# Four attention layers on one core: first heads scored from 16 rows of Q, and one layer's gate moved into the output weights

## Chip, cores and metric

The kernel runs on one core of a Trainium2 chip. A core has TensorE (PE in the tables, with PEld for its weight loads), VectorE (DVE), ScalarE (ACT), GpSimd (POOL) and SyncE (SP, which issues the DMAs), and each runs its own list of instructions. The metric is the time of one execution in microseconds of device time; lower is better.

## The reference

Input x is 2048 tokens by 512 features, one batch. Four layers follow each other, A, B, A, B, each as x = x + layer(layernorm(x)). Both kinds have 32 heads of 16 features.

- Layer B is plain attention over all 2048 tokens: softmax(q k^T / 4) v, then a product with the output weights.
- Layer A works in 4 segments of 512 tokens. Inside a segment it is causal attention. Beside it, a memory M (16 x 16 per head) and a vector z are summed over the earlier segments, and a gate g per head, the sigmoid of beta, mixes the two:

```python
logits = jnp.einsum('bhqd,bhkd->bhqk', qs, ks) * scale + mask
p = _softmax(logits, axis=-1)
a_dot = jnp.einsum('bhqk,bhkd->bhqd', p, vs)
pq = phi(qs)
num = jnp.einsum('bhld,bhde->bhle', pq, M)
den = jnp.einsum('bhld,bhd->bhl', pq, z)[..., None] + 1e-06
a_mem = num / den
o = g * a_mem + (1.0 - g) * a_dot
outs.append(o)
pk = phi(ks)
M = M + jnp.einsum('bhld,bhle->bhde', pk, vs)
z = z + jnp.einsum('bhld->bhd', pk)
```

## The kernel before

The program is a builder: Python code that writes out every engine's instruction list in advance, in an order chosen by a planner with its own costs (`Sched`). Layers are numbered 0 to 3; layers 0 and 2 are A, layers 1 and 3 are B.

**Scores and exponentials.** Heads are handled in groups. Q and K lie in SBUF with features on the partitions, 128 partitions (8 heads) to a channel block c, in QA and KA for A layers and QB and KB for B layers. The array of TensorE is used in four tiles of 32 rows; a tile r holds two heads of 16 features. A group is one segment of queries, one block c and e = 0 or 1, the first or the second head of every tile. To score one head from 32 rows, `select` makes a masked copy `qm` of the Q block, in which the rows of the other head are zero (line 1533); it runs on DVE for A groups and mostly on POOL for B groups. There are 6 such buffers (`NQM`), so three pairs. `unit` then writes two or three score tiles of 128 keys by 512 queries into PSUM banks and lets ACT take their exponential in one instruction of 1024 or 1536 columns into `pT` (line 1643). On the causal diagonal of A groups a mask is added by TensorE (tri, ident) or applied afterwards by POOL (line 1657).

**DVE takes a part of the exponentials.** For chosen score tiles, `dx_first` (line 1165) turns a tile of PSUM into a 16-bit integer that, read as bf16, is a rough power of two; two further passes (lines 1219 and 1236) make two shifted copies, and TensorE adds three products with V in place of one. The buffers for it are `dxt` and parts of KA, QA, VA, wA and wB that are not in use.

**Values.** `pv` multiplies the exponentials with V into one accumulator bank. For B groups the result is 17 rows per head (the 17th is the softmax's sum) in four column tiles of 32; DVE copies it (`ub`), a DMA transposes it (`tb`), and POOL divides it into `ob` (line 1788). For A groups DVE divides (line 1738). A DMA transposes `ob` into `oT`.

**Memory of A layers.** `task_mem` sums phi(K) V into M, then writes masked bf16 copies `Mn` and `Mz`, one instruction each for every block c (lines 884 and 886). For segments 1 to 3 it multiplies them with `phq`, the phi of Q, scales the result by g over the denominator (`amem`), and a DMA transposes it back into `phq`.

**Output of A layers.** `task_out` first gates: for every block c, DVE writes oT = oT * (1 - g) + phq in place (line 994; in segment 0, without memory, oT = oT * (1 - g), line 990). Then, for each of 4 row tiles, `mm_wide` multiplies the 4 blocks with the output weights `woA`, as 4 matmuls of 32 columns of the array each, and DVE adds the result to x (line 1009).

**Background work.** Projections, layer norms (`normalize`, line 695), memory, outputs and DVE's exponentials are tasks that the planner puts between the units of scores. Its limits come from the table `PLAN`, with one row for each stretch of 40 units. `evac` copies projections out of PSUM on DVE, or on ACT where DVE is planned to be late (lines 559 and 561). `keep_busy` and `fill_gaps` put products of a tile of zeros with woB into gaps of TensorE, so that its clock stays up; how much a running product counts for that is set by constants such as `ROW_TILE` and `ROW_FILL`.

Of the kernel before, what the change touches and what calls it, by code (L numbers as in the profile page):

```python
# [7 lines left out]
ALU = mybir.AluOpType  # L8

P = 128  # L10
S_TOK = 2048
D = 512
H = 32
NT = 16
NCH = 4
# [13 lines left out]
ROW_FILL, COL_FILL, COL_ANY, CLOCK = 0.33, 0.15, 0.71, 341  # L29

# [276 lines left out]
class Builder:  # L307
    STRETCH = 40
    PLAN = {
        0: dict(TAKEN_A=1, MASK_PE=800, PE_LOW=7, GAP=3, BG_BANK=400),  # L310
        1: dict(R_LATE=1200, BUSY_ROOM=300, CARRY_W=0, NEARW=40, PAIRS=999, LEVEL=3, TAKEN=0.5, DVE_LATE=1700, BUSY_BACK=800),
        2: dict(MARGIN=500, DX_BANK=900, NEAR=8, EARLY=300, FILL=0.42, CR_B=1200, PART=3, NEARW=20, PAIRS=60, DX_FIN=3000),
        3: dict(NEAR=8, TAKEN_A=1, PV_SKIP=900, BACK=8, CR_W=1900, NEARW=20, TAKEN=0.4, LOW=14, HOLD_AT=40, PHI_LATE=0),
        4: dict(R_LATE=1200, NEARW=40, PAIRS=24, LEVEL=3, TAKEN=0.5),
        5: dict(DX_LATE=700, SLACK=350, BACK=4, LEVEL=3, BUSY_WAIT=0, PE_LOW=7, DVE_LATE=1700),
        6: dict(NEAR=10, PV_SKIP=200, BACK=3, DX_LAG=3, MASK_PE=800, DIV_LATE=2500, BG_BANK=100, QUAD=0),
        7: dict(REST=10, SLACK=350, R_NEAR=10, EARLY=0, FILL_DVE=200, BUSY_ROOM=300, R_PAIRS=2, PAIRS=999, TAKEN=0.3, QWAIT=8, QMIN=4),
        8: dict(R_LATE=1200, BACK=2, CR_W=1300, NEARW=20, BUSY_WAIT=0, TAKEN=0.3, DVE_LATE=800, QWAIT=3, QMIN=4, HOLD_MAX=0, PHI_LATE=300),
        9: dict(ACT1=400, R_LATE=1200, DX_BANK=700, NEAR=18, CR_W=1900, CR_B=1800, R_PAIRS=2, PAIRS=24, DIV_LATE=800, DVE_LATE=800),
        10: dict(DX_LATE=500, NEAR=5, TAKEN_A=1, SLACK=250, CARRY_W=0, R_PAIRS=2, PAIRS=999, DIV_LATE=800, BUSY_WAIT=0, PE_LOW=4, DVE_LATE=800, BG_BANK=100, QUAD=0, HOLD_MAX=0, PHI_LATE=300),  # L320
        11: dict(DX_LATE=900, R_NEAR=10, BUSY_ROOM=900, FILL=0.42, OPART=4, MASK_PE=800, DIV_LATE=2500, DVE_LATE=800, QWAIT=3, QMIN=4, HOLD_SEGS=2, PHI_LATE=0, POOL_QM=1),
# [32 lines left out]
    PHI_LATE = 100  # L354
    LAG_M = 2
    LOOK, PV_TAKEN = 1, 1
    NQM = 6
    NEARW = 60
    WARM, WARM2 = 84, 20
    LAG_A = 2  # L360
# [1736 lines left out]
```

## Time and profile before

| | |
|---|---|
| median of 3 runs | 1741.07 us (1740.86 to 1743.66) |
| the profiled execution | 1743.75 us |
| its span, first to last instruction | 1742.0 us |
| mean granted TensorE clock in it | 0.998 |
| DVE, idle in the span | 12% |
| POOL, busy in the span | 10% |

The profile is of one execution. Busy time counts every moment in which an engine has at least one instruction running, so it can be less than the count times the mean length of one. The rows of the table by stage give, for each engine, busy us and the number of instructions, then the granted clock, the busy share of the DMA engines and GB/s. A row of the view of waits gives who waited, for whom, us in total, how often, and the longest. A row of the groups gives the line, the engine, the operation, what is written from what, the shapes, the count, then busy us, mean ns of one, and the idle time of the engine just before, with what ended it. A row of the timeline has the start and the length in us, and in brackets the idle time before it and its cause.

### The profile page before, as it was taken

To read this page: it belongs to the slowest core of one execution; us is meant where nothing else is said; L and a number is where in the kernel's file an instruction comes from. 1 tells how busy PE (TensorE), PEld (TensorE's weight loads), DVE (VectorE), ACT (ScalarE), POOL (GpSimd) and SP (SyncE) were. 2 spreads that over 40 slices of the span, in tenths; PEclk is the share of its full clock that TensorE was granted. 3 is DMA by queue.
4 is the path that set the end of the run, shared out by engine and by line. 5 is a ranking of instruction groups with operands and counts; after the bars stand their busy time and mean duration, and the time that the engine had idled before them with its cause. 6 is when DMAs were issued, how large, how long until landed. Compare 5 with 4: busy or idle time off the path is not lost.

```text
span 1742.0 us, 47805 instructions
## 1 busy us (share of the span) xinstructions
PE 1652.7 (95%) x19946; PEld 604.6 (35%) x19946; DVE 1527.2 (88%) x2977; ACT 1703.7 (98%) x1608; POOL 182.8 (10%) x292
## 2 busy tenths in 40 slices
PE   8999899999999899999999999999999999999999
PEld 5553335332222523522235222532222222222236
DVE  6758665999999688799998999889999999999996
ACT  7899999999999999999999999999999999999998
POOL 2310100111100300100002100110010100000000
PEclk9999999999999999999999999999999999999999
DMA  6110211001221221102202111010011001000010
GB/s 176 37 22 20 44 14 29 17 8 22 41 47 23 56 56 32 33 8 59 59 14 38 46 32 41 19 46 14 10 23 26 22 13 23 10 10 11 8 29 18
DMA packets 148440, 54.60 MB, mean 31 GB/s; under 512 B 128768, under 2 KB 147712, under 8 KB 148224
## 3 DMA queue, kind: packets, MB, share of 16 engines
q1 hardware_dynamic: 148224, 51.56, 13.9%
q8 instruction: 156, 2.56, 0.6%
q14 instruction: 60, 0.49, 0.1%
HBM read 18.88 MB, written 2.10 MB: 12 GB/s over the span
## 4 chain that ended last, share of the span: by engine, by line
ACT 43%; PE 36%; issue 11%; DVE 6%; DMA 2%; SPq 1%; POOL 1%; ACTq 0%; DVEq 0%; POOLq 0%
ACT pT L1643 42%; PE ps L522 35%; PE ps L2032 1%; SPq L568 1%; DVE KA L1165 1%; DMA tb<-ub 1%; DMA xT<-xn 1%; POOL pT L1657 1%; DVE dxt L1165 1%; ACT amem L762 0%; DVE wA L1165 0%; DVE lnst L667 0%; POOL qm L1533 0%; DMA phq<-amem 0%; DVE VB L561 0%
## 5 line engine op out<-in xcount | busy, mean ns | idle before, releaser
L1643 ACT ACTIVATE pT<-ps 128x1024 bf16<-128x1024 f32 (+1 forms) x1561 | 1670.8, 1239 | 25.3 <-PE ps L522 19.4
L522 PE MATMUL ps<-qm,KB 32*128 32x512 bf16 x4096 | 571.0, 384 | 56.2 <-ACT pT L1643 43.7
L522 PE MATMUL ps<-pT,VB 128*17 128x512 bf16 x2907 | 497.4, 384 | 1.5 <-DVE QB L561 0.3
L522 PEld LDWEIGHTS ps<-qm,KB 32*128 32x128 bf16 x4096 | 148.4, 91 | 561.0 <-ACT pT L1643 462.0
L1165 DVE TENSOR_SCALAR KA<-ps 128x512 uint16<-128x512 f32 (+1 forms) x453 | 315.3, 704 | 11.4 <-PE ps L522 7.6
L1165 DVE TENSOR_SCALAR dxt<-ps 128x512 uint16<-128x512 f32 (+1 forms) x315 | 220.7, 704 | 12.5 <-PE ps L522 9.7
L522 PEld LDWEIGHTS ps<-pT,VB 128*17 128x17 bf16 x2907 | 116.6, 87 | 287.5 <-issue 274.3
L522 PE MATMUL ps<-dxt,VB 128*17 128x512 bf16 x939 | 197.5, 381 | 0.0
L2032 PE MATMUL ps<-woB,zero 128*32 128x512 bf16 (+7 forms) x655 | 166.9, 295 | 0.0
L522 PE MATMUL ps<-QA,VB 128*17 128x512 bf16 x445 | 129.5, 382 | 0.0
L1165 DVE TENSOR_SCALAR wA<-ps 128x512 uint16<-128x512 f32 (+1 forms) x174 | 123.2, 718 | 3.6 <-PE ps L522 1.1
L1788 POOL TENSOR_TENSOR ob<-tb,rd 128x512 bf16<-128x512 bf16 x31 | 35.7, 1152 | 817.9 <-DVE rd L1784 762.4
L522 PE MATMUL ps<-VA,VB 128*17 128x512 bf16 x445 | 120.3, 381 | 0.0
L1657 POOL TENSOR_SCALAR_AFFINE_SELECT pT<-pT 128x256 bf16<-128x256 bf16 (+4 forms) x113 | 61.7, 561 | 480.8 <-ACT pT L1643 480.8
L522 PE MATMUL ps<-KA,VB 128*17 128x512 bf16 x445 | 109.7, 381 | 0.0
L522 PE MATMUL ps<-wA,VB 128*17 128x512 bf16 x555 | 109.0, 381 | 0.0
L522 PE MATMUL ps<-VA,pT 128*128 128x51 bf16 (+1 forms) x2540 | 104.2, 187 | 4.7 <-POOL pT L1657 2.3
L522 PE MATMUL ps<-qm,KA 32*128 32x128 bf16 (+2 forms) x1536 | 93.1, 255 | 12.8 <-ACT pT L1643 9.4
L522 PEld LDWEIGHTS ps<-VA,pT 128*128 128x128 bf16 x2540 | 89.6, 96 | 23.2 <-issue 7.6
L1533 POOL TENSOR_SCALAR qm<-QB,par 128x512 bf16<-128x512 bf16 x96 | 74.0, 780 | 217.6 <-PE ps L522 197.7
L522 PE MATMUL ps<-woB,zero 128*32 128x512 bf16 (+1 forms) x282 | 92.7, 381 | 0.0
L1165 DVE TENSOR_SCALAR wB<-ps 128x512 uint16<-128x512 f32 (+1 forms) x109 | 81.2, 749 | 3.3 <-PE ps L522 2.4
(165 smaller groups left out, 1979.7 us busy)
## 6 DMA issues: line engine op xcount, KB each, us to landing
wB<-in_B_wqkv_dram SPq DMA_DIRECT2D x48, 128.0 KB, 2.3
wA<-in_A_wk_dram SPq DMA_DIRECT2D x16, 128.0 KB, 2.2
wA<-in_A_wq_dram SPq DMA_DIRECT2D x16, 128.0 KB, 2.4
wA<-in_A_wv_dram SPq DMA_DIRECT2D x16, 128.0 KB, 2.5
out_dram<-x SPq DMA_DIRECT2D x8, 256.0 KB, 2.2
x<-in_A_x_dram SPq DMA_DIRECT2D x3, 512.0 KB, 9.8
wB<-in_B_wqkv_dram SPq DMA_DIRECT2D x1, 1536.0 KB, 12.5
oT<-ob SPq DMA_TRANSPOSE x63, 2.4
```

Source lines behind the costliest of these rows:

```text
L522: self.sc.add("pe", lambda e: e.matmul(out, lhsT, rhs, start=start, stop=stop, skip_group_check=True), reads=reads, banks=[(bank, "w", all ...
L568: t[2] = self.sc.add_dma("sp", lambda e: e.dma_start_transpose(out, in_), b, reads=reads, writes=writes, deps=list(deps) + ([t[2]] if t[2] ...
L1165: self.op("dve", lambda e: e.tensor_scalar(d, o, SCALE * LOG2E * 128, 127.0 * 128 + EXP_BIAS, op0=ALU.mult, op1=ALU.add), writes=[self.b_d ...
L1533: self.op(eng, (lambda m, q, col: lambda e: e.tensor_scalar(m, q, col, 0.0, op0=ALU.mult, op1=ALU.add))(m, q, col), reads=[bq, self.b_par] ...
L1643: self.sc.add("act", (lambda dst, src: lambda e: e.activation(dst, src, ACT.Exp, scale=SCALE))(dst, src), writes=self.b_pT[slot * 3 + i:sl ...
L1657: self.op("pool", (lambda blk, pat: lambda e: e.affine_select(blk, blk, pattern=pat, compare_op=ALU.is_ge, fill=0.0, base=0, channel_multi ...
L1788: self.op(eng, lambda e: e.tensor_tensor(ob, t[:, :, :, 0:16], rb, ALU.mult), reads=[br] + self.b_tb, writes=self.b_ob[oi], **(dict(ns=125 ...
L2032: new = Op("pe", 0, (lambda o, z, w: lambda e: e.matmul(o, z, w, start=False, stop=False, skip_group_check=True))(o, z, w), f"fill {cols} ...
```

## The change

1. The first head of each tile (e = 0) gets no masked copy: `scores` and `query` take its 16 rows of Q and of K directly. The second head still uses a copy and 32 rows. `NQM` goes from 6 to 3, and `select` from needing two free copies to needing one. Line numbers move by a few.
2. In layer 2, for blocks 0 to 2 (`NG`), the gate is folded into a scaled copy `woG` of the output weights, made once by DVE. The memory part `phq` of these blocks is no longer added by DVE, but multiplied with `woA` by TensorE into the same accumulation: 7 products per row tile in place of 4 in segments 1 to 3. Block 3 of layer 2 and all of layer 0 stay as they were.
3. `Mn` and `Mz` are written for two blocks c per instruction.
4. 39 of the 40 rows of `PLAN` are replaced, some with settings that no row had before, such as `POOL_XN` (normalization on POOL) in six of them. Only the first row is shown.

```diff
+GATED, NG = 2, 3
...
-        0: dict(TAKEN_A=1, MASK_PE=800, PE_LOW=7, GAP=3, BG_BANK=400),
...
+        0: dict(R_LATE=2200, DX_LATE=500, DX_BANK=900, REST=16, NEAR=18, R_NEAR=50, PV_SKIP=200, CR_W=1900, CR_B=1800, RGAP=2, R_PAIRS=2, PAIRS=24, MASK_PE=800, DIV_LATE=800, PE_LOW=7, DVE_LATE=1700, BG_BANK=100, POOL_QM=1),
...
-    NQM = 6
+    NQM = 3
...
+        self.woG = sb("woG", [P, NG, D], bf)
...
-            for c in range(NCH):
-                hn = bcast(self.hmask[:, 0:1], [[1, 8], [0, 16]])
-                yield [], 0, 500
-                self.op("dve", (lambda c, hn: lambda e: e.tensor_tensor(self.Mn[:, c, :, :], self.M[:, c, :, 0:16], hn, ALU.mult))(c, hn),
-                        reads=[self.b_M[c // 2], self.b_hm], writes=[self.b_Mn], ns=305)
-                self.op("dve", (lambda c: lambda e: e.tensor_tensor(self.Mz[:, c, :], self.M[:, c, :, 16], self.hmask[:, :], ALU.mult))(c),
-                        reads=[self.b_M[c // 2], self.b_hm], writes=[self.b_Mz], ns=160)
+            for j in range(2):
+                hn = bcast(self.hmask[:, 0:1], [[0, 2], [1, 8], [0, 16]])
+                hz = bcast(self.hmask[:, 0:1], [[0, 2], [1, 8]])
+                yield [], 0, 600
+                self.op("dve", (lambda j, hn: lambda e: e.tensor_tensor(self.Mn[:, 2 * j:2 * j + 2, :, :], self.M[:, 2 * j:2 * j + 2, :, 0:16], hn, ALU.mult))(j, hn),
+                        reads=[self.b_M[j], self.b_hm], writes=[self.b_Mn], ns=450)
+                self.op("dve", (lambda j, hz: lambda e: e.tensor_tensor(self.Mz[:, 2 * j:2 * j + 2, :], self.M[:, 2 * j:2 * j + 2, :, 16], hz, ALU.mult))(j, hz),
+                        reads=[self.b_M[j], self.b_hm], writes=[self.b_Mz], ns=200)
...
+            if L == GATED and s == 0 and ti == 0:
+                for c in range(NG):
+                    yield [("attn", 0, 3), self.later()], 0, 400
+                    self.op("dve", (lambda c: lambda e: e.tensor_scalar(self.woG[:, c, :], self.woA[:, c, :], self.gfm[:, c:c + 1], 0.0, op0=ALU.mult, op1=ALU.add))(c),
+                            reads=[self.b_gfm, self.b_woA], writes=[self.b_woG], ns=390)
             if isA and ti == 0:
 
-                for c in range(NCH):
+                for c in range(NG if L == GATED else 0, NCH):
                     o, m, gc = self.oT[:, 0, c, :], self.phq[:, c, :], self.gfm[:, c:c + 1]
...
             k = L % 2
-            srcs = [(self.oT[:, k, c, :], c, [self.b_oT[k][c]]) for c in range(NCH)]
+            ng = NG if L == GATED else 0
+            srcs = [(self.oT[:, k, c, :], (self.woG if c < ng else wo)[:, c, :], [self.b_oT[k][c], self.b_woG if c < ng else bwo]) for c in range(NCH)]
+            if s:
+                srcs += [(self.phq[:, c, :], wo[:, c, :], [self.b_phq[c], bwo]) for c in range(ng)]
             for n, (a, c, ba) in enumerate(srcs):
-                if half and n == self.OPART:
-                    yield ["cont"], NCH - n, 700
+                if n in ((self.OPART, self.OPART + NCH) if half else (NCH,)):
+                    yield ["cont"], min(len(srcs) - n, NCH), 700
                 self.bg_cols += 512
-                self.mm_wide(bank, a[:, ti * 128:(ti + 1) * 128], wo[:, c, :], n == 0, n == len(srcs) - 1, list(ba) + [bwo], al)
+                self.mm_wide(bank, a[:, ti * 128:(ti + 1) * 128], c, n == 0, n == len(srcs) - 1, list(ba), al)
...
-        while len(self.qm_free) > 1:
+        while len(self.qm_free) > 0:
...
-                g.qm = self.qm_free.pop(0)
-                isA = g.kind == "A"
-                q = (self.QA[:, self.aslot(g.L, g.qseg), g.c, :] if isA else self.QB[:, g.qseg, g.c, :])
-                bq = (self.b_QA[self.aslot(g.L, g.qseg)][g.c] if isA else self.b_QB[g.qseg][g.c])
-                m = self.qm[:, g.qm, :]
-                col = self.par[:, g.e:g.e + 1]
-                eng = "dve" if late or not self.POOL_QM and (isA or any(h.kind == "A" for h in self.sel)) else "pool"
-                self.op(eng, (lambda m, q, col: lambda e: e.tensor_scalar(m, q, col, 0.0, op0=ALU.mult, op1=ALU.add))(m, q, col),
-                        reads=[bq, self.b_par], writes=[self.b_qm[g.qm]], ns=762 if eng == "pool" else 386, gap=720 if eng == "pool" else 300)
+                if g.e:
+                    g.qm = self.qm_free.pop(0)
+                    isA = g.kind == "A"
+                    q = (self.QA[:, self.aslot(g.L, g.qseg), g.c, :] if isA else self.QB[:, g.qseg, g.c, :])
+                    bq = (self.b_QA[self.aslot(g.L, g.qseg)][g.c] if isA else self.b_QB[g.qseg][g.c])
+                    m = self.qm[:, g.qm, :]
+                    col = self.par[:, g.e:g.e + 1]
+                    eng = "dve" if late or not self.POOL_QM and (isA or any(h.kind == "A" for h in self.sel)) else "pool"
+                    self.op(eng, (lambda m, q, col: lambda e: e.tensor_scalar(m, q, col, 0.0, op0=ALU.mult, op1=ALU.add))(m, q, col),
+                            reads=[bq, self.b_par], writes=[self.b_qm[g.qm]], ns=762 if eng == "pool" else 386, gap=720 if eng == "pool" else 300)
                 self.sel.insert(at + i, g)
...
-                self.qm_late.append(self.sel.pop(0).qm)
+                g = self.sel.pop(0)
+                if g.e:
+                    self.qm_late.append(g.qm)
...
+    def query(self, g, r, q0, n):
+
+        if g.e:
+            return slice(32 * r, 32 * r + 32), self.qm[32 * r:32 * r + 32, g.qm, q0:q0 + n], self.b_qm[g.qm]
+        rows = slice(32 * r, 32 * r + 16)
+        if g.kind == "A":
+            sl = self.aslot(g.L, g.qseg)
+            return rows, self.QA[rows, sl, g.c, q0:q0 + n], self.b_QA[sl][g.c]
+        return rows, self.QB[rows, g.qseg, g.c, q0:q0 + n], self.b_QB[g.qseg][g.c]
+
+    def scores(self, g, what, r, bank, first, second):
+
+        if g.kind == "A":
+            sl = self.aslot(g.L, g.qseg)
+            parts = [(g, p) for p in PARTS[what]] + ([(g.mate, p) for p in PARTS["k2m"]] if what == "k2" else [])
+            for m, (h, (kb, off, N, q0)) in enumerate(parts):
+                rows, q, bq = self.query(h, r, q0, N)
+                (first if m == 0 else second[m - 1]).append((self.ps[:, bank.col0 + off:bank.col0 + off + N],
+                                                             self.KA[rows, sl, g.c, kb * 128:(kb + 1) * 128], q, m == 0,
+                                                             [self.b_KA[sl][g.c], bq], bank, r, N))
+            return
+        ks, kk = self.kslot(g.L, what // 4), what % 4
+        rows, q, bq = self.query(g, r, 0, 512)
+        first.append((self.ps[:, bank.col0:bank.col0 + 512], self.KB[rows, ks, g.c, kk * 128:(kk + 1) * 128], q, True,
+                      [self.b_KB[ks][g.c], bq], bank, r, 512))
+
...
+            self.scores(g, what, r, u[i], first_mm, second_mm)
...
+            self.scores(g, what, r, bank, first_mm, second_mm)
```

More of the change, by code (lines that the diff above doesn't have):

```diff
@@ L309 @@
     PLAN = {
-        0: dict(TAKEN_A=1, MASK_PE=800, PE_LOW=7, GAP=3, BG_BANK=400),
[L311 to L319, printed above, removed]
@@ L458, in alloc @@
         self.b_wB = n2("wB", 3, NCH)
-        self.b_woA, self.b_woB = B("woA"), B("woB")
+        self.b_woA, self.b_woB, self.b_woG = B("woA"), B("woB"), B("woG")
         self.b_KB = n2("KB", self.NKS, NCH)
```

103 lines of the change are left out of this document (40 added, 63 removed).

## The prediction

> **What bounds the kernel now.** I read the page first, for the share of each engine, and then the table of busy time by stage, cut where the layers change.
>
> ```profile
> span 1742.0 us, 47805 instructions
> PE 1652.7 (95%) x19946; PEld 604.6 (35%) x19946; DVE 1527.2 (88%) x2977; ACT 1703.7 (98%) x1608; POOL 182.8 (10%) x292
> ```
>
> ```profile
> core 0: us, PE busy (x) PEld busy (x) DVE busy (x) ACT busy (x) POOL busy (x), PEclk, DMA share, GB/s
> 0.00:131.00 131.00, 119.58 (x1775) 68.74 (x1779) 83.57 (x217) 113.00 (x96) 32.48 (x74) 0.99 0.30 78
> 131.00:566.00 435.00, 410.36 (x4852) 145.09 (x4850) 364.09 (x742) 429.52 (x382) 41.81 (x63) 1.00 0.14 26
> 566.00:741.00 175.00, 164.40 (x2340) 75.23 (x2344) 139.68 (x312) 171.38 (x151) 23.26 (x39) 1.00 0.21 44
> 741.00:871.00 130.00, 124.08 (x1317) 35.60 (x1313) 123.73 (x240) 128.93 (x127) 6.60 (x10) 1.00 0.19 42
> 871.00:1176.00 305.00, 293.95 (x3688) 110.84 (x3680) 274.46 (x533) 302.85 (x282) 37.38 (x62) 1.00 0.15 34
> 1176.00:1698.00 522.00, 500.49 (x5133) 142.66 (x5130) 510.94 (x878) 520.00 (x537) 39.86 (x43) 1.00 0.08 17
> 1698.00:1742.00 44.00, 39.80 (x869) 26.44 (x868) 30.76 (x61) 37.99 (x39) 1.37 (x1) 0.98 0.06 18
> ```
>
> ACT (ScalarE) works through the exponentials of the scores and is busy for 98% of the span. Its idle time is 38.3 us: 18.0 before 131 us, 6.0 in the tail, and 14.3 in the five stages between (5.48, 3.62, 1.07, 2.15 and 2.00). So a change can pay in two ways only: ACT gets fewer columns, or ACT stands less. The view of waits says what it stands for:
>
> ```profile
> ACT pT L1643 <- PE ps L522: 19.4, 43, 1.7
> ...
> PE ps L522 <- ACT pT L1643: 53.1, 180, 1.2
> ...
> PE ps L522 <- DVE qm L1533: 2.5, 2, 1.4
> ```
>
> ACT stands for score matmuls that come late. PE in turn mostly waits for ACT to free a bank; DVE's masked query qm, which the change takes away for half of the groups, holds it up for 2.5 us at two places.
>
> **ACT's own work.** I compared the instruction lists of the two built programs. The settings of 39 of the 40 stretches are new, yet the split of the exponentials hardly moves: DVE takes 1104 tiles of 512 columns before and 1106 after. ACT's instructions of 1024 columns go from 1051 to 1023, those of 1536 from 510 to 528, and it gets 4 more copies out of PSUM (one VA, two KA, one ub).
>
> ```profile
> L1643 ACT ACTIVATE pT<-ps 128x1024 bf16<-128x1024 f32 x1051 | 1006.0, 1111 | 5.2 <-PE ps L522 3.1
> L1643 ACT ACTIVATE pT<-ps 128x1536 bf16<-128x1536 f32 x510 | 728.1, 1502 | 20.2 <-PE ps L522 16.3 <-POOL pT L1657 1.2 <-POOL VB L923 0.3
> ```
>
> Busy time over count is 0.957 us for the narrow form and 1.428 for the wide one (the instructions overlap, so the mean of one, 1111 or 1502 ns, is too long as a price). That gives -28 x 0.957 + 18 x 1.428 = -1.1 us, and 4 copies at 0.60 us, the length of ACT's copy of QA at 12.18 us below, are +2.4: **+1.3 us**. The ends are -1.1, if the copies fall into idle time, and +2.4.
>
> **The masked query.** Before, each pair of heads needs two masked copies of Q, made on DVE or POOL between the Q projection and its first scores. After, the first head is scored from its own 16 rows of Q and K, and only the second head's copy remains. Two places show a copy on the path that feeds ACT. The first is the start:
>
> ```profile
> 12.18 0.60 ACT L559 ACTIVATE QA<-ps 128x512 bf16<-128x512 f32 x1 [2.27 <-PE ps L522]
> 12.81 0.61 DVE L1533 TENSOR_SCALAR qm<-QA,par 128x512 bf16<-128x512 bf16 x2 [0.80 <-ACT QA L559]
> 13.22 0.39 PE L522 MATMUL ps<-qm,KA 32*128 32x512 bf16 x3 [1.08 <-DVE qm L1533]
> ```
>
> Without the copy the scores can start where the copy starts now: 13.22 - 12.81 = 0.41, **-0.4 us** (0 if something else is late there). The second is near 80 us (first the row of that stage in the table by stage, then the timeline):
>
> ```profile
> 80.00:87.00 7.00, 5.95 (x89) 3.36 (x89) 3.12 (x8) 4.19 (x4) 2.26 (x4) 0.76 0.31 63
> ```
>
> ```profile
> 79.77 0.63 ACT L559 ACTIVATE QA<-ps 128x512 bf16<-128x512 f32 x1
> 79.98 0.87 POOL L1657 TENSOR_SCALAR_AFFINE_SELECT pT<-pT 128x768 bf16<-128x768 bf16 x1 [1.06 <-ACT pT L1643]
> 80.03 1.22 DVE L1533 TENSOR_SCALAR qm<-QA,par 128x512 bf16<-128x512 bf16 x2
> 81.05 0.61 PE L522 MATMUL ps<-qm,KA 32*128 32x512 bf16 x3 [1.39 <-DVE qm L1533]
> ...
> 82.14 1.45 ACT L1643 ACTIVATE pT<-ps 128x1536 bf16<-128x1536 f32 x1 [1.74 <-PE ps L522]
> ```
>
> PE stands 1.39 us for the copies, its granted clock falls to 0.76 in these 7 us, the scores take 0.61 instead of 0.39 us, and ACT is busy for 4.19 of 7.00: 2.81 us lost. Without the copy the scores can begin at the end of the Q copy, 79.77 + 0.63 = 80.40 instead of 81.05: 0.65 won for certain if the order stays, and all of 2.81 if the clock holds. I take the middle, **-1.7 us**. What is late next is the Q copy itself, which both kernels have.
>
> A clock of 0.76 over 7 us is a deficit of 1.68 us, or 3.4 us at half speed. [...]
>
> The 16-row scores themselves are not in the trace. Their tile in the array stays 32 x 128, they stream as many columns, and rows show that the row count does not set the price:
>
> ```profile
> L522 PE MATMUL ps<-qm,KB 32*128 32x512 bf16 x4096 | 571.0, 384 | 56.2 <-ACT pT L1643 43.7 <-DVE KA L1165 3.2 <-DVE wA L1165 2.2
> L522 PE MATMUL ps<-wA,xT 128*128 128x512 bf16 x48 | 12.8, 379 | 2.2 <-DVE VA L561 1.2 <-ACT VA L559 1.0
> ```
>
> 384 ns for 32 rows, 379 for 128: I take 0. That Q tiles are now read until their last score costs nothing either: the projections that overwrite them wait in both kernels for that segment's attention to be finished.
>
> **DVE and POOL get lighter.** Counts from the two lists, prices from these rows:
>
> ```profile
> L1165 DVE TENSOR_SCALAR KA<-ps 128x512 uint16<-128x512 f32 x436 | 294.8, 683 | 9.6 <-PE ps L522 6.0
> L1165 DVE TENSOR_SCALAR KA<-ps 128x1024 uint16<-128x1024 f32 x17 | 20.8, 1221 | 1.8 <-PE ps L522 1.6
> ...
> L695 DVE TENSOR_SCALAR xn<-x,lnst,lnw 128x512 bf16<-128x512 bf16 x60 | 23.9, 419 | 2.3 <-DMA xT<-xn 2.0
> L1533 DVE TENSOR_SCALAR qm<-QA,par 128x512 bf16<-128x512 bf16 x58 | 19.7, 382 | 0.9 <-ACT QA L559 0.8
> L994 DVE SCALAR_TENSOR_TENSOR oT<-oT,gfm,phq 128x512 bf16<-128x512 bf16 x24 | 17.8, 745 | 3.8 <-DMA phq<-amem 3.7
> L884 DVE TENSOR_TENSOR Mn<-M,hmask 128x128 bf16<-128x128 f32 x24 | 7.6, 316 | 0.0
> L1533 POOL TENSOR_SCALAR qm<-QB,par 128x512 bf16<-128x512 bf16 x96 | 74.0, 780 | 217.6 <-PE ps L522 197.7 <-DVE QB L561 10.6 <-DVE xn L695 8.4
> ```
>
> DVE: 41 query copies fewer at 0.34 us (19.7/58), -13.9; 20 normalizations moved to POOL at 0.398, -8.0; 9 gated sums of layer 2 fewer at 0.742, -6.7; three plain gatings replaced by three scalings of the output weights, 0; the masked memory matrices in 12 instructions of double width instead of 24, between 0 and half of 7.6, taken as -2; 4 copies gone to ACT, about -2.7 at 0.683; 5 divisions come from POOL, +3.7 at the 0.742 of the gated sum. First passes over the scores: 60 narrow ones fewer and 31 wide ones more, -41.0 + 37.9 = -3.1, which the added second passes (14 more, some narrower) about give back. In all about -30 of 1527 us. POOL: 47 - 3 = 44 copies fewer at 0.77, -34, and 20 normalizations at no less than that price, +15; 16 masks fewer.
>
> None of this is on the path by itself; it shortens waits of PE for DVE. So the 14.3 us of idle ACT between 131 and 1698 us bounds the gain: from 0 to -14.3. I take a quarter, **-3.6 us**, nearer to 0 because ACT's waits name PE, and PE's work grows.
>
> POOL's new work has a price for DVE: near 80 us two copies that take 0.34 us each elsewhere took 1.22 while POOL ran its mask. [...]
>
> **Layer 2's output.** The gate goes into scaled weights for three of four channel blocks, and the memory part, which DVE added, becomes three more accumulating products for each of 12 row tiles: 144 matmuls of 32 columns of the array.
>
> ```profile
> L522 PE MATMUL ps<-woA,oT 128*32 128x512 bf16 x448 | 36.7, 380 | 0.0
> ```
>
> ```profile
> 871.00:1176.00 305.00, 31.16 (x116) 10.18 (x116) 0.00 (x0) 0.00 (x0) 1.00 0.15 34
> ```
>
> At 36.7/448 = 0.082 us that is +11.8 us of PE. The second row, the same stage for the tile of zeros alone, shows the cover: 31.2 us of PE there are filler products that only keep the clock up. I cost it at 0; if the filler can't give way, up to +11.8. The scaling of the weights is three DVE instructions once in the run, with DVE 10% idle in that stage.
>
> **The sum.** 1742.0 + 1.3 - 0.4 - 1.7 - 3.6 = 1737.6 us of span. The profiled execution took 1743.75 us, 1.75 above its span; the median of the runs is 1741.07, which is 0.93 below that span. I carry this 0.93 over: 1736.7, and say **1736.5 us**, 0.26% faster. (About 0.2%, 3.5 us, is what can be told from no change.)
>
> **Rivals.**
>
> *Hidden anyway.* DVE's relief reaches nobody, since PE mostly waits for ACT (53.1 against 2.5 for qm). Then only the sure parts count: 1742.0 + 1.3 - 0.4 - 0.65 - 0.93 = 1741.3, no change. For it: the split of the exponentials did not move, so ACT's work is the same. Against it: the two places above are real stops of ACT.
>
> *The clock (the other side).* Half of the scores now use 16 rows of the array instead of 32, and the weights with which the builder decides on filler products are unchanged. If the activity that keeps the clock up counts rows, places with little filler drop to half speed, as at 80 us: before 131 us and where the memory layers run. One such place costs up to the 2.81 us shown. Two cancel the gains of 5.7; four give 1736.5 + 11.2 = 1747.7. For it: filler is hardly more than before (349 thousand columns against 346). Against it: the clock is 1.00 in all middle stages, so how far it is from the edge can't be seen.
>
> *PE becomes the bound in layer 2.* The 11.8 us are not covered: 1736.5 + 11.8 = 1748.3. Against it: 31.2 us of filler in that stage. [...]
>
> *Better feeding throughout.* All idle time of the middle goes and the clock holds at 80 us: 1742.0 - 1.1 - 0.4 - 2.8 - 14.3 - 0.9 = 1722.5. For it: new settings in every stretch; against it: PE's waits for ACT are of the pipeline's own making.
>
> **How the numbers follow.** Forecast 0.43 (its own range 1731 to 1738), better feeding 0.11, hidden anyway 0.25, clock 0.14, PE in layer 2 0.07. Faster by over 0.2%: 0.11 and 0.41 of the forecast's, 0.52. Same: 0.25 and 0.02, the forecast's upper edge, 0.27. Slower: 0.21. The range has to reach towards both sides; from 1724 to 1747 it leaves out the far end of better feeding and the upper half of the slower cases, 2 in 10 together.
>
> **What would show it.** ACT busy within 2 us of 1705 with 1023 and 528 exponentials; no PE wait for qm near 80 us and a clock of 1.00 there; the first exponential 0.4 us earlier; ACT's idle time between 131 and 1698 us near 11 instead of 14; the gated sum x15; less filler from 871 to 1176 us with ACT's idle unchanged there. A mean clock under 0.99, or stages under 1.00 in the middle, would make the clock rival right. The prediction is wrong if ACT's busy time itself moves by more than 3 us.

## The result, and the profile after

| | before | after |
|---|---|---|
| median | 1741.97 us (6 runs) | 1754.49 us (6 runs, 1750.98 to 1757.39) |
| ratio to before | | 1.0068 [1.0053, 1.0082] |
| the profiled execution | 1743.75 us | 1750.98 us |
| its span | 1742.0 us | 1749.2 us |
| mean granted clock of the runs | 0.998 in the profiled one | 0.994 to 0.998 |

The change makes the kernel 0.7% slower, about 12.5 us. The profiled execution of after is the fastest of its six runs, and that of before (1743.75 us) is slower than before's median, so the two profiles show only 7.2 us of that. What the other runs of after lose more is seen in a second profile of the same kernel, below.

First the page's own lines, the groups of exponentials, and the waits of ACT and PE for each other. The last row of waits is from before, for comparison:

```profile
span 1749.2 us, 47828 instructions
...
PE 1655.1 (95%) x20036; PEld 605.5 (35%) x20106; DVE 1504.4 (86%) x2869; ACT 1705.9 (98%) x1602; POOL 183.1 (10%) x247
```

```profile
L1654 ACT ACTIVATE pT<-ps 128x1024 bf16<-128x1024 f32 x1023 | 985.1, 1099 | 11.0 <-PE ps L525 8.4 <-ACT pT L1654 0.3
L1654 ACT ACTIVATE pT<-ps 128x1536 bf16<-128x1536 f32 x528 | 756.8, 1494 | 18.3 <-PE ps L525 14.7 <-POOL pT L1668 0.5 <-ACT pT L1654 0.2
```

```profile
PE ps L525 <- ACT pT L1654: 53.7, 175, 1.7
ACT pT L1654 <- PE ps L525: 23.2, 53, 4.4
PE ps L525 <- DMA xT<-xn: 5.5, 4, 3.4
```

```profile
PE ps L522 <- DMA xT<-xn: 3.4, 3, 1.4
```

DVE is 22.8 us lighter, POOL is as heavy as before, ACT has 2.2 us more to do. ACT's wait for scores did not shrink with DVE's load: it went from 19.4 to 23.2 us, the longest single wait from 1.7 to 4.4. PE's wait for the transposed normalization (`xT<-xn`) grew from 3.4 to 5.5 us, its longest from 1.4 to 3.4. The table by stage says where (us, then busy us and instructions of PE, PEld, DVE, ACT, POOL, then the clock, DMA share and GB/s):

```profile
0.00:131.00 131.00, 117.78 (x1747) 69.53 (x1772) 77.82 (x194) 115.34 (x98) 29.53 (x66) 1.00 0.30 78
131.00:566.00 435.00, 407.36 (x4935) 145.50 (x4944) 366.92 (x734) 430.11 (x384) 35.02 (x49) 1.00 0.14 25
566.00:741.00 175.00, 166.22 (x2313) 74.02 (x2324) 135.16 (x273) 170.74 (x151) 41.67 (x47) 1.00 0.24 46
741.00:871.00 130.00, 125.98 (x1308) 35.78 (x1305) 123.31 (x229) 128.51 (x128) 14.28 (x12) 1.00 0.16 38
871.00:1176.00 305.00, 290.75 (x3689) 109.86 (x3703) 253.43 (x486) 296.33 (x270) 32.15 (x47) 0.99 0.14 30
1176.00:1698.00 522.00, 501.08 (x5072) 140.68 (x5072) 509.76 (x879) 520.21 (x531) 29.04 (x27) 1.00 0.09 19
```

Length less ACT's busy time is its idle time: 15.66, 4.89, 4.26, 1.49, 8.67 and 1.79 us. Before 131 us that is 2.3 less than before; in the five middle stages it is 21.1 instead of 14.3, and 6.5 of the growth lie in one stage, 871 to 1176 us. There one place stands out (timeline; DMA_TRANSPOSE writes xT for the projections):

```profile
874.98 4.50 POOL L698 TENSOR_SCALAR xn<-x,lnst,lnw 128x512 bf16<-128x512 bf16 x2 [4.64 <-DVE lnw L689]
877.49 10.14 SPq L571 DMA_TRANSPOSE xT<-xn  x4
...
881.68 4.74 POOL L698 TENSOR_SCALAR xn<-x,lnst,lnw 128x512 bf16<-128x512 bf16 x2 [2.21 <-DMA xT<-xn]
...
889.10 1.90 PE L525 MATMUL ps<-xT,wA 128*32 128x512 bf16 x16 [3.36 <-DMA xT<-xn]
890.93 0.61 PE L525 MATMUL ps<-qm,KB 32*128 32x512 bf16 x3
...
891.64 1.02 ACT L1654 ACTIVATE pT<-ps 128x1024 bf16<-128x1024 f32 x1 [4.41 <-PE ps L525]
```

```profile
885.00:890.00 5.00, 1.64 (x20) 0.63 (x22) 1.55 (x4) 2.23 (x2) 2.08 (x2) 0.75 0.39 79
890.00:895.00 5.00, 5.00 (x48) 1.11 (x40) 2.14 (x5) 2.47 (x2) 0.00 (x0) 0.56 0.02 5
```

POOL needs 4.5 and 4.7 us for two normalizations each. The last transposition is late by that, PE stands for 3.36 us in front of a projection that was already next in its list, the clock is at half for some 6.8 us (0.50 from 888 to 894 us, a mean of 0.83 from 880 to 900 us), and ACT loses 5.3 us of these 10. The group rows give the price on the two engines, beside POOL's query copy:

```profile
L698 POOL TENSOR_SCALAR xn<-x,lnst,lnw 128x512 bf16<-128x512 bf16 x20 | 45.4, 2275 | 105.9 <-DVE lnw L689 96.2 <-DMA xT<-xn 9.5 <-POOL xn L698 0.2
L698 DVE TENSOR_SCALAR xn<-x,lnst,lnw 128x512 bf16<-128x512 bf16 x40 | 15.8, 416 | 0.9 <-DMA xT<-xn 0.7
L1546 POOL TENSOR_SCALAR qm<-QA,par 128x512 bf16<-128x512 bf16 x9 | 6.5, 720 | 0.9 <-DVE QA L564 0.9
```

The same tile costs 2.28 us on POOL and 0.42 on DVE; the copy with one scalar per partition, 0.72 on POOL, is no measure for the normalization, which takes two scalars per partition (which of its differences makes it long was not tested). The planner's own cost for it is 0.8 us.

### The profile page after: what moved, and what is told of

Read it like the earlier page. It is cut to its first block, busy times and chain, and to the rows that moved or that the text cites. A ratio compares the mean times of both kernels' runs of the same rounds, so it can differ in the third digit from the quotient of the medians.

```text
span 1749.2 us, 47828 instructions
## 1 busy us (share of the span) xinstructions
PE 1655.1 (95%) x20036; PEld 605.5 (35%) x20106; DVE 1504.4 (86%) x2869; ACT 1705.9 (98%) x1602; POOL 183.1 (10%) x247
## 4 chain that ended last, share of the span: by engine, by line
ACT 38%; PE 35%; DVE 11%; issue 11%; DMA 3%; POOL 1%; SPq 1%; ACTq 0%; DVEq 0%; POOLq 0%
ACT pT L1654 38%; PE ps L525 34%; DVE KA L1177 3%; DVE dxt L1177 2%; DMA tb<-ub 1%; DMA xT<-xn 1%; PE ps L2043 1%; DVE wA L1177 1%; POOL xn L698 1%; SPq L571 1%; DVE dxt L1231 1%; DVE lnst L670 0%; DVE wB L1177 0%; ACT amem L765 0%; DVE QA L1231 0%
## 5 line engine op out<-in xcount | busy, mean ns | idle before, releaser
L1654 ACT ACTIVATE pT<-ps 128x1024 bf16<-128x1024 f32 (+1 forms) x1551 | 1671.3, 1233 | 29.2 <-PE ps L525 23.2
L525 PE MATMUL ps<-QB,KB 16*128 16x512 bf16 x2048 | 373.6, 384 | 29.5 <-ACT pT L1654 21.4
L525 PE MATMUL ps<-qm,KB 32*128 32x512 bf16 x2048 | 364.8, 385 | 27.8 <-ACT pT L1654 22.1
L1177 DVE TENSOR_SCALAR dxt<-ps 128x512 uint16<-128x512 f32 (+1 forms) x344 | 245.2, 717 | 14.1 <-PE ps L525 10.2
L525 PE MATMUL ps<-dxt,VB 128*17 128x512 bf16 x1050 | 224.7, 382 | 0.0
L525 PEld LDWEIGHTS ps<-qm,KB 32*128 32x128 bf16 x2048 | 90.7, 91 | 286.3 <-ACT pT L1654 233.1
L525 PEld LDWEIGHTS ps<-QB,KB 16*128 16x128 bf16 x2048 | 92.7, 91 | 280.3 <-ACT pT L1654 222.5
L2043 PE MATMUL ps<-woB,zero 128*32 128x512 bf16 (+7 forms) x495 | 130.1, 301 | 0.1
L525 PE MATMUL ps<-woB,zero 128*32 128x512 bf16 (+1 forms) x353 | 114.7, 381 | 0.4
L1177 DVE TENSOR_SCALAR wA<-ps 128x512 uint16<-128x512 f32 (+1 forms) x150 | 110.6, 745 | 3.2 <-PE ps L525 2.2
L1231 DVE TENSOR_SCALAR dxt<-dxt 128x1024 uint16<-128x1024 uint16 (+1 forms) x226 | 89.7, 424 | 1.3
## 6 DMA issues: line engine op xcount, KB each, us to landing
wB<-in_B_wqkv_dram SPq DMA_DIRECT2D x1, 1536.0 KB, 12.5
```

The lines of the kernel that those rows point to most:

```text
L525: self.sc.add("pe", lambda e: e.matmul(out, lhsT, rhs, start=start, stop=stop, skip_group_check=True), reads=reads, banks=[(bank, "w", all ...
L1177: self.op("dve", lambda e: e.tensor_scalar(d, o, SCALE * LOG2E * 128, 127.0 * 128 + EXP_BIAS, op0=ALU.mult, op1=ALU.add), writes=[self.b_d ...
L1231: self.op("dve", (lambda d, s, c: lambda e: e.tensor_scalar(d, s, float(c), None, op0=ALU.add))(d, s, c), reads=[self.b_dxt[b][0]], writes ...
L1654: self.sc.add("act", (lambda dst, src: lambda e: e.activation(dst, src, ACT.Exp, scale=SCALE))(dst, src), writes=self.b_pT[slot * 3 + i:sl ...
L2043: new = Op("pe", 0, (lambda o, z, w: lambda e: e.matmul(o, z, w, start=False, stop=False, skip_group_check=True))(o, z, w), f"fill {cols} ...
```

## Experiments

In all of them but runs 6 and 7, the order in which each engine works is that of the kernel they start from: the costs and dependences that the planner sees were left as they were. Of each edit only the lines that matter are shown. Runs 1 to 4, 8, 9 and 10 were made on one chip, runs 5 to 7 on another; before, measured beside them, had medians of 1741.82 (runs 1 to 4), 1741.68 (5 to 7) and 1742.61 us (8 to 10).

**1. The normalizations back on DVE (label e1_xn_dve).** After, with the 20 normalizations planned at POOL's cost and issued on DVE:

```diff
-  writes=[self.b_xn[n]], **(dict(ns=800, gap=760) if eng == "pool" else dict(ns=448)))
+  writes=[self.b_xn[n]], place="dve", **(dict(ns=800, gap=760) if eng == "pool" else dict(ns=448)))
```

> The changed kernel with its 20 POOL normalizations put back on DVE, every other instruction in the same order. Theory 1 (POOL's normalization takes 2.2 us where DVE's takes 0.4, and near 889 us a projection waits 3.4 us for it, with 6.8 us of half clock behind): the stall of ACT of 4.4 us near 891 us and the half clock there are gone, the time falls by 5 to 9 us from 1754.5, to about 1747. Theory 2 (scores of 16 rows count less for the clock): time and clock stay within 3 us and 0.002 of the changed kernel. Theory 3 (the new order of work is worse all over): within 3 us of it, too.

Measured: 1750.3 us (8 runs, 1745.9 to 1761.14), 1.0051 [1.0031, 1.0071], against 1754.4 for after on the same chip (below). The wait of 4.4 us is gone. The runs spread over 15 us, and go with the clock: 1745.9 at 0.999, 1748.43 at 0.997, 1754.03 at 0.993, 1761.14 at 0.986. By the medians POOL's normalizations cost some 4 us, but the intervals of the two ratios overlap (run 4 has [1.0056, 1.009]). The stage with the stall shows it without the spread: 4.12 us of idle ACT from 871 to 1176 us, where after had 8.67.

```profile
871.00:1176.00 305.00, 294.24 (x3752) 110.92 (x3749) 259.18 (x500) 300.88 (x274) 22.32 (x42) 1.00 0.15 32
```

Something else takes the clock away in the slow ones of these runs.

**2. Before, with 16 rows (label e2_rows16_before).** The first head's scores use the upper 16 rows of the masked copy and of K; the copies stay.

```diff
-            rows = slice(32 * r, 32 * r + 32)
+            rows = slice(32 * r, 32 * r + (32 if g.e else 16))
```

> The kernel before, with all its masked copies, but the first heads scored from the upper 16 rows of copy and K: same instructions in the same order, only the row count of half of the score matmuls differs. Theory 1 and theory 3: no change, 1740 to 1744 us, clock 0.998. Theory 2: 4 to 12 us slower, with a mean clock of 0.994 to 0.996 in most runs.

Measured: 1743.93 us (11 runs, 1742.07 to 1748.28), 1.0016 [1.0006, 1.0026]. The two slowest runs, both 1748.28, had clocks of 0.995 and 0.993; those at 1742.07 had 1.0 and 0.999. Nothing but the number of rows differs from before, so 16 rows cost about 2 us here, and the runs with the full clock lose least.

**3. After, with 32 rows (label e3_rows32_after).** The first head is scored without a copy but from all 32 rows, so its scores hold the sum of both heads; other values, but the same instructions.

```diff
-        rows = slice(32 * r, 32 * r + 16)
+        rows = slice(32 * r, 32 * r + 32)
```

> The changed kernel with the first heads scored from 32 rows of Q and K without a mask (so these scores are sums over two heads), same instructions in the same order. Theory 2: the clock goes back to 0.998 in all runs and the time falls by 3 to 8 us from 1754.5. Theories 1 and 3: within 2 us of the changed kernel, and its runs still spread over 6 us with clocks from 0.994 to 0.998.

Measured: 1749.6 us (5 runs, 1748.84 to 1753.69), 1.0047 [1.0034, 1.006], with clocks of 0.997 to 0.999. The stall of the normalizations is still there: ACT idles 8.57 us from 871 to 1176 us.

**4. After once more (label c_after),** for a second profile and a comparison on the same chip.

> The changed kernel again, on the chip of the three runs above, as their base: 1751 to 1757 us, clock 0.994 to 0.998. All theories expect the stall near 891 us in its profile.

Measured: 1754.4 us (6 runs, 1750.4 to 1759.5), 1.0073 [1.0056, 1.009], clocks from 0.992 to 0.998. The 32 rows of run 3 are worth 4.8 us by the medians, DVE's normalizations of run 1 4.1; with these spreads neither step alone is clear of the noise. This time the profiled execution is a long one, 1758.38 us with a clock of 0.992. Stretches of it, and of the run with DVE's normalizations (second fence), where both are at the same work:

```profile
core 0: us, PE busy (x) PEld busy (x) DVE busy (x) ACT busy (x) POOL busy (x), PEclk, DMA share, GB/s
950.00:957.00 7.00, 5.87 (x91) 2.82 (x91) 3.31 (x9) 7.00 (x7) 0.00 (x0) 1.00 0.09 19
957.00:967.00 10.00, 10.00 (x76) 1.97 (x77) 6.08 (x9) 7.36 (x7) 0.00 (x0) 0.50 0.13 28
967.00:977.50 10.50, 10.50 (x65) 2.42 (x61) 6.43 (x10) 6.77 (x7) 0.00 (x0) 0.50 0.22 38
977.50:985.00 7.50, 7.02 (x80) 2.15 (x77) 7.32 (x14) 7.07 (x7) 0.00 (x0) 1.00 0.05 11
```

```profile
957.00:967.00 10.00, 9.80 (x106) 2.94 (x99) 9.85 (x16) 9.88 (x12) 0.00 (x0) 1.00 0.24 53
967.00:977.50 10.50, 9.85 (x122) 2.92 (x122) 9.21 (x17) 10.40 (x11) 0.00 (x0) 1.00 0.23 64
```

In the first, the clock is at half for 20.5 us, though PE is busy all the time and ACT, just before, has no gap at all. ACT does 14.1 us of work in these 20.5 and loses 6.4. One such spell explains most of the distance between the executions at 0.992 and at 0.998, whose spans differ by 7.4 us. Two rows of the timeline, one from just before it and one from within, have products of one shape at 0.38 and at 0.63 us:

```profile
955.59 0.38 PE L525 MATMUL ps<-KA,VB 128*17 128x512 bf16 x1
...
957.79 0.63 PE L525 MATMUL ps<-QA,VB 128*17 128x512 bf16 x1
```

**5. Both at once (label e4_both):** normalizations on DVE and 32 rows.

> Both undone at once in the changed kernel: normalizations back on DVE and first heads from 32 unmasked rows (so these scores are sums over two heads); order of all instructions kept. If theories 1 (POOL's normalization) and 2 (the clock) add up: 1754.4 - 4.1 - 4.8 = 1745.5 us, clock 0.998 or more in every run. If they are the same loss seen twice (the late projection only hurts through the clock): about 1749.5, as with either alone. What is left above 1741.8 belongs to the new order of work (theory 3).

Measured: 1746.61 us (8 runs, 1745.6 to 1747.08), 1.0025 [1.0015, 1.0035]. All eight clocks are 0.999 or 1.0, and the spread is 1.5 us instead of 15. The two losses together are 7.8 us of after's 12.6; 4.9 are left. The interval is clear of that of after. The full clock is not without exception, though: the profiled execution (clock 0.999) has one short stretch at half speed, near 217 us (first row), which run 10, with the same 32 rows, does not have (second row):

```profile
215.00:222.00 7.00, 6.31 (x63) 2.21 (x64) 3.21 (x8) 5.76 (x5) 0.00 (x0) 0.76 0.10 19
```

```profile
215.00:222.00 7.00, 5.77 (x72) 2.28 (x72) 4.56 (x10) 6.76 (x6) 0.00 (x0) 1.00 0.21 15
```

**6. More filler (label e6_fill).** Run 1, with a 16-row score counted as half a score where the builder decides on products of the tile of zeros: 1057 of them in place of 866.

```diff
-            edge[k][int(at // 10)] += 1
+            part = .5 if name == "half" else 1
+            edge[k][int(at // 10)] += part
```

> The changed kernel with normalizations on DVE (base: 1750.3 us, clock 0.986 to 0.999) and, in the pass that puts products of zeros into gaps, 16-row scores counted at half the weight of 32-row ones: 1057 fillers of 396 thousand columns instead of 866 of 349 thousand, all else in the same order. Theory 2: the clock returns to 0.998 or more and the time falls by 3 to 5 us, to about 1746. Rival: fillers take PE's time, and it stays at 1750 or gets slower, even if the clock rises.

Measured: 1755.37 us (6 runs, 1746.68 to 1764.63), 1.0077 [1.0052, 1.0102], clocks 0.985 to 0.998. A miss: the additional products did not hold the clock. That they made it worse is not shown, the interval overlaps that of run 1. The same spell is there (first row of the first fence); the row of the tile of zeros alone (second fence: PE, PEld, ACT, POOL, then the clock) shows that few of them run in it, 2.89 us of 21, and PE has no gap there. So this run tells nothing of what filler in the right place would do. The profiled execution, 1764.63 us, is the slowest of the six, and it has two more spells, both in layer 3, behind the memory layers (the other rows):

```profile
955.00:960.00 5.00, 5.00 (x41) 1.26 (x38) 2.20 (x5) 3.48 (x3) 0.00 (x0) 0.50 0.13 26
1340.00:1350.00 10.00, 10.00 (x85) 2.65 (x80) 8.29 (x13) 8.15 (x8) 0.00 (x0) 0.70 0.09 19
1720.00:1730.00 10.00, 10.00 (x155) 6.45 (x151) 6.66 (x14) 6.86 (x7) 0.00 (x0) 0.50 0.01 2
```

```profile
953.00:974.00 21.00, 2.89 (x7) 0.70 (x8) 0.00 (x0) 0.00 (x0) 0.51 0.16 36
```

ACT idles 6.6, 2.7 and 6.4 us more than in run 1's profile in the stages of the three spells (871 to 1176, 1176 to 1698, and from 1698 us on).

**7. The settings tables exchanged.** After's code with before's `PLAN` (label e8_old_plan), and before's code with after's `PLAN`, normalizations on DVE (label e9_new_plan).

> The changed kernel with the table of settings of before (no normalization on POOL; the planner orders the work anew). Theory 3, new settings at fault: 1740 to 1745 us. If the edits themselves (16 rows, layer 2's output) carry the rest of the loss: 1748 or more. Theory 2 expects clocks below 0.998 in some runs in either case.

> The kernel before with the new table of settings, normalizations kept on DVE (the planner orders the work anew). Theory 3, new settings at fault: 1745 to 1750 us. If the edits carry the loss: 1740 to 1744. Theory 2: the clock is 0.998 or more in all runs, since all scores have 32 rows.

Measured: 1775.16 us (4 runs), 1.0193 [1.0177, 1.0209], and 1781.26 us (5 runs), 1.023 [1.0217, 1.0243], both far outside what was expected. Each table is slow with the other's code, so the 4.9 us can't be split between code and table in this way. Inconclusive for that question.

**8. The removal of the copies alone (labels e11_bare32 and e13_bare16).** Before, in its own order, without the first heads' copies. Their scores wait for Q instead, and still for the instruction that stood ahead of the copy on its engine. In e11_bare32 they use 32 rows and hold the sum of both heads, in e13_bare16 16 rows as in the change (the lines shown are of the latter).

```diff
+    def bare(self, g):
+        return g.e == 0
...
+    def rows(self, g, r):
+        return slice(32 * r, 32 * r + (16 if self.bare(g) else 32))
...
+        if g.kind == "A":
+            sl = self.aslot(g.L, g.qseg)
+            return self.QA[rows, sl, g.c, q0:q0 + n], [self.b_qm[g.qm], self.b_QA[sl][g.c]]
+        return self.QB[rows, g.qseg, g.c, q0:q0 + n], [self.b_qm[g.qm], self.b_QB[g.qseg][g.c]]
```

> The kernel before, in its own order, with one part of the change: the masked copies of all first heads are left out, and those heads are scored straight from Q and K. They use 32 rows here, not 16, so a first head's scores hold the sum of both heads of the tile; what is left is the removal of 77 copies without any change in rows used. If the removal is worth what my steps said (0.4 us at the start, 0.65 to 2.8 near 80 us, and for the relief of DVE and POOL about half of the 3.6 us, as about 14 of some 30 us of DVE's relief are copies): 1741.9 - 0.4 - 1.7 - 1.7 = 1738.1 us. If DVE's and POOL's relief reaches nobody: 1741.9 - 0.4 - 1.7 = 1739.8, at worst 1740.9. If what after loses beyond the clock and POOL's normalizations comes from the removal of copies itself: over 1742.

> As the run with the bare first heads, but from 16 rows, as the change does it: the first part of the change alone, in the order of before. The two runs differ in the rows alone. Theory (16 rows cost by the clock): 2 to 5 us over the run with 32 rows, as in the two pairs measured so far (+2.1 in the kernel before, +4.8 in the kernel after), so 1740 to 1744 us, with a granted clock below 0.998. Rival (rows cost nothing in this order): the same time as the run with 32 rows.

Measured: with 32 rows 1742.51 us (12 runs), 1.0007 [0.9996, 1.0017]; with 16 rows 1748.22 us (9 runs, clocks 0.991 to 0.998), 1.0033 [1.0019, 1.0047]; before 1742.61 (32 runs). The page of the first:

```profile
PE 1651.7 (95%) x19946; PEld 603.8 (35%) x19946; DVE 1517.1 (87%) x2943; ACT 1703.5 (98%) x1608; POOL 144.0 (8%) x241
```

85 copies are gone (34 on DVE, 51 on POOL; the expectation says 77). DVE is 10.1 us lighter than before, POOL 38.8, and the time is the same. The profiles say where the start and the place near 80 us went: ACT idles 2.0 us less than before up to 131 us, and 2.3 more from 566 to 741 us, where this execution has a stretch at a clock of 0.93 (616 to 641 us, 2.98 us of idle ACT instead of 0.89). In the other four middle stages together it idles 9.7 us instead of 10.7, so at most about 1 us of the relief can have reached ACT. The rows then cost 5.7 us by the medians (0.0026 by the ratios, 4.5 us).

**9. Only layer 0's first heads bare, from 16 rows (label e12_bare16_first).**

```diff
-        return g.e == 0
+        return g.e == 0 and g.L == 0
```

> The kernel before with only layer 0's first heads scored bare from 16 rows; all other groups keep their copies and their 32 rows. The order is that of before. Theory: the gain at the start and near 80 us comes (0.4 + 1.7), the clock's price stays out because nearly all scores keep 32 rows: 1739.8 us, below both kernels. Rival 1: the two places are made good later (ACT's work is the same and something else is late): 1741 to 1742. Rival 2: the 16 rows cost clock in the first 131 us already: 1742 to 1745.

Measured: 1740.66 us (12 runs, 1739.42 to 1742.03), 0.999 [0.9981, 1.0]: the lowest of all kernels run here, 1.95 us under before by the medians, though the interval reaches 1.0; clocks 0.998 to 1.0 (before 0.996 to 1.0). The stage near 80 us, in this run:

```profile
80.00:87.00 7.00, 6.12 (x106) 3.43 (x104) 3.73 (x12) 5.79 (x5) 2.29 (x4) 1.00 0.49 96
```

The clock is whole there, and ACT busy for 5.79 instead of 4.19 us. In this profile ACT idles 0.8 us less than before up to 131 us, 0.7 less from 131 to 566 us (layer 0's scores run until 303 us), and 0.95 less in the four stages behind, whose groups the edit leaves as they were. So only a part of the 1.95 us can be placed at the start and near 80 us.

**10. Layer 2's memory products cut short (label e10_short_mem).** Run 5 with 64 of the 512 columns in each of the 144 products of `phq` with `woA`; only these 64 columns get their memory part.

```diff
-  self.mm_wide(bank, a[:, ti * 128:(ti + 1) * 128], c, n == 0, n == len(srcs) - 1, list(ba), al)
+  self.mm_wide(bank, a[:, ti * 128:(ti + 1) * 128], c, n == 0, n == len(srcs) - 1, list(ba), al, 64 if n >= NCH else 512)
```

> The run with the normalizations on DVE and 32 unmasked rows (1746.61 us), with layer 2's 144 products of the memory part and the output weights cut from 512 to 64 columns, so only 64 columns get their memory part; order and fillers unchanged. It takes 144 x 0.082 x 7/8 = 10.3 us of matmul time from PE. My step (hidden, 0): the same time within 1 us, 1745.6 to 1747.6. The rival (PE is the bound in layer 2): up to 10 us less, and if it explains what is left over before: 1741.7.

Measured: 1745.42 us (12 runs), 1.0017 [1.0008, 1.0025]. The first row is the group in after, the second in this run:

```profile
L525 PE MATMUL ps<-woA,phq 128*32 128x512 bf16 x144 | 12.9, 380 | 0.0
```

```profile
L528 PE MATMUL ps<-woA,phq 128*32 128x64 bf16 x144 | 6.0, 194 | 0.0
```

PE is relieved of 6.9 us (a narrow product still takes 194 ns, so less than the 10.3 expected), and 1.2 us of it, within the two intervals' width, arrive in the time. ACT's idle time from 871 to 1176 us falls by about as much, from 4.14 us in run 5 to 3.10. The products are mostly hidden.

## Why the prediction was wrong, and where it was right

Three steps of the prediction failed: the 16-row scores, taken at 0, cost some 4 us, with granted clocks of 0.986 to 0.999 in run 1 against 0.999 to 1.0 in run 5; the normalizations on POOL, taken as a relief, cost some 3 to 4 us in a wait for the projections; and the relief of -3.6 us hardly came. What the runs say of the 12.6 us between before and after:

| | us | from |
|---|---|---|
| 16 rows, with lower clocks | 3.7 to 4.8 | run 1 less run 5, and run 4 less run 3 |
| normalizations on POOL | 3.0 to 4.1 | run 3 less run 5, and run 4 less run 1 |
| left in run 5 over before | 4.9 | 1746.61 less 1741.68 |

In the first two rows one of the two differences compares runs on different chips, and the intervals of most of these pairs touch or overlap: the sizes are rough, the two causes rest on the clocks and on the stage from 871 to 1176 us. The last row is the sum of gains and losses; the two profiled executions differ by only 3.0 us (1745.0 - 1742.0), as that of before was a slow one. In the profile of run 5 ACT is busy for 1706.0 us, 2.3 more than before; it idles 3.8 us less before 131 us, and 4.3 us more in the five middle stages, 18.6 against 14.3:

```profile
131.00:566.00 435.00, 407.69 (x4914) 144.66 (x4912) 366.37 (x738) 428.26 (x383) 25.43 (x42) 1.00 0.15 25
566.00:741.00 175.00, 166.97 (x2323) 73.93 (x2318) 135.12 (x278) 169.71 (x150) 24.24 (x40) 1.00 0.23 47
741.00:871.00 130.00, 126.04 (x1326) 36.31 (x1322) 123.63 (x234) 129.32 (x129) 4.68 (x8) 1.00 0.15 38
871.00:1176.00 305.00, 294.42 (x3747) 110.89 (x3745) 259.27 (x500) 300.86 (x274) 23.00 (x44) 1.00 0.15 32
1176.00:1698.00 522.00, 501.12 (x5080) 140.68 (x5078) 509.95 (x877) 520.22 (x532) 28.53 (x27) 1.00 0.08 18
```

Point by point:

- **The bound** was read rightly: ACT stays at 98%, and every loss found ends as idle time of ACT in front of late scores.
- **ACT's own work**, +1.3 us, came as +2.2, inside the bounds of -1.1 and +2.4. The four copies came at about their price, but the exponentials, priced at -1.1, came as +0.5 (1670.8 to 1671.3 us, both forms together). The counts 1023 and 528 are as foreseen.
- **The start**, -0.4 us: ACT now waits 0.58 us after the Q copy where it waited 0.88, so -0.3. The first exponential did not come earlier in these two profiles, at 13.84 instead of 13.66 us, because the Q copy itself came 0.48 us later.
- **The place near 80 us**, -1.7 us. Its row in after:

```profile
80.00:87.00 7.00, 6.34 (x111) 3.63 (x114) 2.48 (x9) 5.93 (x6) 2.07 (x5) 1.00 0.43 83
```

  1.07 us lost instead of 2.81: -1.74, with the clock whole, as predicted, where before has it at 0.50 from 81 to 84 us. But the size was luck. Run 2 keeps the copies and the order of before, and PE waits for them as long (first row); its clock is whole there all the same, and ACT loses 1.64 us (second row, the same 7 us of work, which came 1.34 us later):

```profile
82.39 0.39 PE L522 MATMUL ps<-qm,KA 16*128 16x512 bf16 x3 [1.39 <-DVE qm L1533]
```

```profile
81.34:88.34 7.00, 5.95 (x109) 3.52 (x109) 3.12 (x8) 5.36 (x5) 2.25 (x4) 1.00 0.49 78
```

  So the copies alone do not bring the clock down at this place, and with the clock whole their removal was worth 1.64 - 1.07 = 0.6 us, near the 0.65 that the prediction had as certain. That run 9 is 1.95 us faster than before, where the two terms together were 2.1, is no proof of them either.
- **"The 16-row scores: I take 0" failed.** The duration was right, 384 against 385 ns in after, but the price was not to be found in the duration:

```profile
L525 PE MATMUL ps<-QB,KB 16*128 16x512 bf16 x2048 | 373.6, 384 | 29.5 <-ACT pT L1654 21.4
L525 PE MATMUL ps<-qm,KB 32*128 32x512 bf16 x2048 | 364.8, 385 | 27.8 <-ACT pT L1654 22.1
```

  Four pairs of kernels that differ in the rows alone gave 2.1, 3.7, 4.8 and 5.7 us, with lower clocks each time (0.993 to 1.0 against 0.997 to 1.0, 0.986 to 0.999 against 0.999 to 1.0, 0.992 to 0.998 against 0.997 to 0.999, 0.991 to 0.998 against 0.997 to 1.0). In the last three the score values differ too, and the 3.7 compares two chips; run 2 against before (2.1) has neither. That is the outcome of the clock rival, which had 0.14; that the clock counts rows is not shown. The rival was right that memory layers are such a place (the long spell lies among layer 2's memory products) and that there can be several, as in run 6, though two of those lie in layer 3; wrong on the first 131 us, where the clock is whole in after, and on the size: a single spell can cost 6.4 us instead of 2.81, in some runs and not in others (957 to 977.5 us is at 0.50 in the second profile of after and at 1.00 in the first). Its sign, a mean clock under 0.99, was set too far off: after's runs are at 0.992 to 0.998.
- **The normalizations on POOL failed** as a term. They were taken for a relief of DVE by 8.0 us, at a price for POOL of "no less than" 0.77 us each. The lower bound was used as the price. They took 2.28, three times that, and the step did not ask who waits for xn: the transposition, then the projections, which stand in PE's list ahead of the next scores. The row for that was in the waits of before, `PE ps L522 <- DMA xT<-xn: 3.4, 3, 1.4`, and was not read.
- **The relief, -3.6 us, failed.** Run 8 takes 10.1 us from DVE and 38.8 from POOL, and the middle stages show at most about 1 us for it; in run 5 ACT's middle idle time grows by 4.3 although DVE is 20.6 us lighter. The rival "hidden anyway" was right on this term. ACT's idle time is a bound of a gain only if what is relieved is what ends the waits, and the waits named PE.
- **Layer 2's output at 0** is nearly right: 1.2 us. But not because filler gave way, as the prediction had it: in that stage it is 28.9 us in after and 31.4 in run 5, which has the same filler, against 31.2 in before. That this filler keeps the clock up was the author's assumption: no run leaves it out, and run 6, with 191 more of these products, had clocks of 0.985 to 0.998 where run 1 had 0.986 to 0.999.
- **What stays open:** of the 4.9 us of run 5, the +2.3 of ACT's work and the 1.2 of the products are accounted for. Of the 1.3 and 1.7 us that ACT stands longer between 131 and 741 us, the 1.3 go with the stretch at half speed near 217 us: runs 3 and 10, which don't have it, idle 4.84 and 5.32 us from 131 to 566 us, less than before. The 1.7 are not settled; the exchange of the tables could not tell new order from new code.

The stretches at half speed differ in length: some 3.4 us near 217 us in run 5 (an estimate from the mean of 0.76 over 7 us), 6.8 us behind the stall in after, 20.5 us in run 4. In the last, PE was busy for 20.50 of 20.50 us at a clock of 0.50. What sets their length is not shown.

## What to carry to other kernels

A product with fewer rows can take the same time (384 and 385 ns here) and still cost (2.1 to 5.7 us in the four pairs): look at the granted clock of several runs, not at the duration. A stretch at half speed in one profile may be absent from the next execution of the same kernel (the 20.5 us at 0.50 in one profile of after are at 1.00 in the other), so do not price a gain from it before a second profile shows it again. Do not take the price of an operation on another engine from a relative with fewer operands (0.72 us for the copy, 2.28 for the normalization on POOL), and ask who waits for its result before calling it a relief. Where one engine is busy for 98%, price lighter work on its neighbours by what the waits name: here that was 0.3 and 0.6 us at the two places where the trace showed the removed copy itself in the wait, and 10.1 us less on DVE and 38.8 on POOL left run 8 at 1742.51 us against 1742.61.

## What the runs showed of the hardware that was not expected

- Score products of 32 x 128 tiles with 16 in place of 32 rows go with a lower granted clock, though they are as long (384 and 385 ns): 0.991 to 0.998 against 0.997 to 1.0 in the two halves of run 8, 0.986 to 0.999 in run 1 against 0.999 to 1.0 in run 5. Why is not shown.
- A half-clock spell can last for 20.5 us with PE busy throughout (run 4, and again in run 6). PE has no gaps in these 20.5 us, and still the clock stays at 0.50. Whether the spell keeps itself up was not tested.
- More filler in the gaps of PE did not prevent such a spell: with 191 more products of zeros in the program the clock was 0.985 to 0.998, and PE was busy for 5.00 of 5.00 us within the spell (955 to 960 us).
- In after, GpSimd took 2.28 us for a 128 x 512 subtract and multiply with two scalars per partition, VectorE 0.42 us (line 698); a multiply and add with one scalar per partition and a constant took GpSimd 0.72 us on QA and 0.85 on QB (line 1546).
